# Linear attention into a gated MLP on one core: a quarter of the hidden layer by seven half products in four more blocks, with the kv and numerator steps moved around it

## The chip, the core and the metric

The kernel runs on one core of a Trainium2 chip. The metric is the device time of one execution in microseconds. Five engines run side by side, each with its own queue in program order: TensorE (PE, its weight loads shown as PEld), VectorE (DVE), ScalarE (ACT), GpSimd (POOL) and SyncE (SP, which here only issues DMAs).

## What is computed

```python
# q, k, v: (8, 8, 576, 64); phi(x) = (x if x > 0 else exp(x) - 1) + 1
kv  = einsum('bhsd,bhse->bhde', phi(k), v)   # per batch and head
num = phi(q) @ kv ; den = phi(q) @ sum_s phi(k) + 1e-6
x   = (num / den) as (4608 tokens, 512)
h   = x @ w_in                        # (4608, 2048)
g   = h * sigmoid(beta * h)
out = g @ w_out                       # (4608, 512), float32
```

## The kernel before

**Blocks.** The 8 batches are taken one after the other. Of each batch's 576 tokens 512 make a block (blocks 0 to 7); the 64 left over go into `xT_tail`, and the eight remainders make block 8. Blocks 0 and 1 are prepared by a written-out prologue. From block 1 on a loop (L1012) runs, per block, an H stage (x times w_in, with Silu into `g_sb`) and then a Y stage (`y_fast`, L904: g times w_out). While block b is in these stages, the attention part of later batches is slipped in between: the loop puts functions into two lists, `sh` for the H stage and `sy` for the Y stage, under the number of the step behind which they run (`at`, `run`, L714 to L719). The order of the instructions on each engine is what this program writes; nothing reorders it.

**The H stage.** The 2048 hidden columns are 16 column blocks `ff` of 128, four to a quarter. `h_phase` (L737, blocks 1 to 6) computes each by four matmuls of 512 tokens (`h_mm`, L395) into one PSUM bank (pool of 4, tag "h"), and ScalarE's Silu (`silu`, L408) empties it. `h_fast` (L805, blocks 7 and 8) computes quarters 0 and 2 otherwise (`products`, L817): the 512 x 512 x 512 product of a quarter is split in halves in all three directions and done with seven half products instead of eight, Strassen's scheme in Winograd's form. Each half product is four matmuls of 256 columns. It needs sums of weight halves (`h_w_sums`, L778, four DVE operations per quarter, once), sums of x halves (`h_x_sums`, L792, four DVE operations per block), and six DVE operations per quarter on the results: copy of the first product (L841), two additions that build on it (L844, L845), c2's upper half (L850), hc's upper half (L855) and c2's lower half (L856). The seven products stand in three parts, each behind one plain column block; `hc` is a tile of two PSUM banks (pool "w", two such tiles), `hz` another; the sums that ScalarE reads lie in `hc` and in `c2`.

**The Y stage.** `y_fast` does out = g w_out by seven half products as well (pa twice, pd twice, pc, pb twice; 16 matmuls of 256 columns each). It needs `g_diff` (L721) and `g_sums` (L725) on DVE from the H stage. Its chain on DVE: u2 = pc + r1 (L968), u3 = pd + u2 (L969), y2 = pb + u3 (L978), y2 = pd + u2 (L981), y1 = pb + u2 (L989). The second product into pd accumulates onto the bank that u3 reads, the second into pb onto the bank that y2 reads. The steps of `sy` run at L961 to L999: step 1 behind the first pd product, step 3 behind u3, step 6 at the end.

**Attention for later batches.** `kv_both(n)` (L212) is 72 small matmuls and one DVE copy; `numer_all(n)` (L318) is 72 small matmuls, then four groups of three DVE operations that write x into `xs_sb` (`evac`, L339), and four transposing DMAs on SP's queue from `xs_sb` to `xT` (`trans`, L352). In blocks 3 to 6 they stand at steps 1 and 4 of the H stage, in block 2 at steps 2 and 5. `tail_copy` (L366, POOL) copies the last 64 tokens of a landed `xT`. `next_loads` (L1001, POOL) issues the loads of v, q and k two batches ahead. In the Y stage phi of q (steps 0 and 1) and of k (steps 3 and 4) of batch b + 2 are made by ScalarE's exponential, DVE's `phi_relu` (L165, into an "r" tile, four buffers) and `phi_min` (L173); `q_trans_dma` (step 1) transposes phi of q through SP's queue.

Of the kernel before, what the change touches and what calls it, by code (L numbers as in the profile page):

```python
# [16 lines left out]
def kernel(  # L17
# [145 lines left out]
        st[b, a, pr, "e"] = e  # L163

    def phi_relu(b, a, pr, x):  # L165
        r = work.tile([P, 2, J, D], BF16, tag="r", name="r", bufs=4)
        nc.vector.tensor_scalar(r, x, 0.0, 1.0, ALU.max, ALU.add)
        st[b, a, pr, "r"] = r

    def phi_tile(b, a):  # L170
        st[b, a] = work.tile([P, 2, J, P], BF16, tag=f"phi{a}", name=f"phi_{a}", bufs=1)
# [542 lines left out]
    def run(side, n):  # L714
        for f in side.get(n, ()):
            f()
# [20 lines left out]
    def h_phase(b, x, side):  # L737
        for ff in range(FC):
# [15 lines left out]
                g_parts(b, ff)  # L754


    h_w = vf.rearrange("p i j d -> p (i j d)").bitcast(BF16)
    h_ws = [
        [h_w[:, (4 * n + k) * 512 : (4 * n + k + 1) * 512].rearrange("p (i f) -> p i f", i=2)
         for k in range(4)] for n in range(2)  # L760
    ]
    h_xs = [
        [xq[n].rearrange("p i j d -> p (i j d)")[:, k * 512 : (k + 1) * 512].rearrange(
            "p (i n) -> p i n", i=2) for k in range(4)] for n in range(2)
    ]
    h_c2 = xk[0].rearrange("p i j d -> p (i j d)").bitcast(F32)[:, 0:1024].rearrange(
        "p (t n) -> p t n", t=2
    )
    h_u = [
        xk[1].rearrange("p i j d -> p (i j d)").bitcast(F32)[:, n * 512 : (n + 1) * 512]  # L770
        for n in range(2)
    ]

    def h_w_plain(fq, f, r):

# [1 line left out]

    def h_w_sums(fq):  # L778

        s, a = h_ws[fq // 2], lambda f, r: h_w_plain(fq, f, r)  # L780
        nc.vector.tensor_add(s[0], a(1, 0), a(1, 1))
        nc.vector.tensor_sub(s[1], s[0], a(0, 0))
        nc.vector.tensor_sub(s[2], a(0, 0), a(1, 0))
        nc.vector.tensor_sub(s[3], a(0, 1), s[1])

    def h_x_plain(b, r, t):

# [1 line left out]
            return xT_tail[:, :, 4 * t : 4 * t + 4, r]  # L789
        return xT[b % 2][:, :, 4 * t + r : 4 * t + 4 : 2]  # L790

    def h_x_sums(b):  # L792

        t = h_xs[b % 2]
        x = lambda r, t: h_x_plain(b, r, t)

        def like(a, c):
            return a.rearrange("p i (t n) -> p i t n", n=c.shape[-1])

        for k, (u, w) in enumerate((  # L800
            (x(0, 1), x(0, 0)), (x(1, 1), t[0]), (x(1, 1), x(0, 1)), (x(1, 0), t[1])
        )):
            nc.vector.tensor_sub(like(t[k], u), u, like(w, u) if k % 2 else w)

    def h_fast(b, x, side):  # L805
        run(side, 0)
        hps_of = {}

        def plain(ff):
            hps_of[ff] = bank("h_ps")  # L810
            h_mm(x, ff, hps_of[ff])

        def act(*ffs):
            for ff in ffs:
                silu(b, ff, hps_of[ff])

        def products(fq):  # L817
            s, t = h_ws[fq // 2], h_xs[b % 2]
            cw, z = banks("hc"), banks("hz")[:, 0]
            c2 = h_c2  # L820

            def product(ps, lhs, rhs, first):
                for a in range(2):
                    for i in range(2):
                        o = ps[:, a * 256 : (a + 1) * 256]
                        m = rhs[:, i]
                        if len(m.shape) > 2:
                            o = o.rearrange("p (t n) -> p t n", n=m.shape[-1])
                        nc.tensor.matmul(  # L829
                            o, lhs[:, i, a * P : (a + 1) * P], m,  # L830
                            start=(first and a == 0 and i == 0), stop=True,
                            skip_group_check=True,
                        )

            def w(f, r):
                return h_w_plain(fq, f, r)

            def part1():
                z6 = bank("hz")
                product(z6, s[1], t[1], True)  # L840
                nc.vector.tensor_copy(h_u[0], z6)  # L841
                product(cw[:, 0], w(0, 0), h_x_plain(b, 0, 0), True)
                product(z, s[2], t[2], True)
                nc.vector.tensor_add(h_u[0], cw[:, 0], h_u[0])  # L844
                nc.vector.tensor_add(h_u[1], z, h_u[0])  # L845

            def part2():
                product(cw[:, 1], s[0], t[0], True)
                product(cw[:, 0], w(0, 1), h_x_plain(b, 1, 0), False)
                nc.vector.tensor_add(c2[:, 1], cw[:, 1], h_u[1])  # L850

            def part3():
                product(cw[:, 1], s[3], h_x_plain(b, 1, 1), False)
                product(z, w(1, 1), t[3], False)
                nc.vector.tensor_add(cw[:, 1], cw[:, 1], h_u[0])  # L855
                nc.vector.tensor_add(c2[:, 0], z, h_u[0])  # L856

            def out(n, parts=range(2)):

                for a in parts:  # L860
                    ff = 4 * fq + 2 * n + a
                    src = (cw, c2)[n][:, :, a * 256 : (a + 1) * 256]
                    nc.scalar.activation(
                        g_sb[b % 2][:, ff].rearrange("p (t n) -> p t n", t=2), src,
                        ACTF.Silu, scale=beta_c[:, ff : ff + 1],
                    )

            return part1, part2, part3, out

        plain(4)  # L870
        act(4)
        p1, p2, p3, out = products(0)
        p1()
        plain(5)
        act(5)
        p2()
        plain(6)
        act(6)
        p3()
        out(0)  # L880
        plain(7)
        act(7)
        out(1)
        plain(12)
        act(12)
        p1, p2, p3, out = products(2)
        p1()
        g_diff(b, slice(0, 4))
        plain(13)
        act(13)  # L890
        p2()
        g_diff(b, slice(4, 8))
        plain(14)
        act(14)
        p3()
        out(0, [0])
        plain(15)
        act(15)
        out(0, [1])
        out(1)  # L900
        g_sums(b, 4, 8)
        g_sums(b, 0, 4)

    def y_fast(b, side):  # L904
# [47 lines left out]

        r1 = work.tile([P, 512], F32, tag="r1", name="r1", bufs=1)
        u2 = work.tile([P, 512], F32, tag="u2", name="u2", bufs=1)
        u4 = work.tile([P, 512], F32, tag="u4", name="u4", bufs=1)
        u3 = work.tile([P, 512], F32, tag="u3", name="u3", bufs=1)
        if b < B - 2:
            table(ACTF.Exp)
# [53 lines left out]
    for b in range(1, B + 1):  # L1012
# [3 lines left out]
            at(sh, 0, lambda: tail_copy(b))  # L1016
        if n < B:
            at(sh, 0, lambda: next_loads(n))
            at(sh, {1: 9, 2: 2}.get(b, 1), lambda: kv_both(n))
            at(sh, {1: 11, 2: 5}.get(b, 4), lambda: numer_all(n))  # L1020
        if b == 1:
            at(sh, 4, lambda: w_sum(2))
            at(sh, 9, lambda: w_sum(1))
# [1 line left out]
        if m < B:  # L1025
# [12 lines left out]
            else:  # L1038
# [2 lines left out]
                at(sy, 1, lambda: q_trans_dma(m))  # L1041
                at(sy, 3, lambda: phi_part(m, "k", 0))
                at(sy, 4, lambda: phi_part(m, "k", 1), lambda: table(ACTF.Silu))
        if b == B - 2:
            at(sh, 0, lambda: h_w_sums(0))
            at(sh, 2, lambda: h_w_sums(2))
            at(sy, 0, lambda: h_x_sums(B - 1))
        if b == B - 1:
            at(sy, 0, lambda: h_x_sums(B))
        (h_phase if b < B - 1 else h_fast)(b, xT[b % 2] if b < B else xT_tail, sh)  # L1050
        y_fast(b, sy)


# [28 lines left out]
```

## Time and profile before

| | us |
|---|---|
| median of 3 runs (275.02 to 275.17) | 275.16 |
| the profiled execution, whole | 275.76 |
| its span in the trace | 274.0 |
| H stages of blocks 3, 4, 5, 6 | 15.56, 15.52, 15.61, 15.62 |
| H stages of blocks 7, 8 | 13.36, 13.35 |
| Y stage of each of blocks 2 to 7 | 12.23 |

The granted TensorE clock is 0.999. A timeline row gives the start in us, the length, engine, line, operation, output and inputs by the program's names, shapes, the number of instructions that were merged, and in brackets the idle time of the engine before it with what ended it. Ends of matmuls are modelled, so a row's length runs past the start of the next; distances from start to start are what is used below.

### The profile page before, as it was taken

The numbers are of one execution on the slowest core, as the hardware profiler recorded it, in microseconds if no ns is written. First come the engines' busy times: TensorE is split into PE (matmuls) and PEld (weight loads), VectorE is DVE, ScalarE is ACT, GpSimd is POOL, SyncE is SP. The second block draws the span as 40 slices with busy tenths as digits, with TensorE's granted clock in tenths as the row PEclk, the third lists the DMA queues.
The fourth block names the chain that finished last, engine by engine and source line by source line (L and its number), as shares of the span: only waits on it lengthen the run. The fifth ranks groups of instructions, "written<-read, shape, count | busy, mean of one in ns | idle before, by whom it ended". The sixth has DMA issues, their size and how long they took to land.

```text
span 274.0 us, 6637 instructions
## 1 busy us (share of the span) xinstructions
PE 266.0 (97%) x2809; PEld 176.6 (64%) x2809; DVE 187.8 (69%) x362; ACT 171.3 (63%) x237; POOL 45.8 (17%) x64
## 2 busy tenths in 40 slices
PE   7899998999999999999999999999999999999994
PEld 2575454445865487548754885488548866886793
DVE  4871785999895677566857684677866467856862
ACT  4838877976777776589457945795573047416710
POOL 5932102043014031230113002310000000000000
PEclk9999999999999999999999999999999999999999
DMA  7999999557998996994599659985531060023013
GB/s 253 237 206 350 257 385 255 174 102 228 217 114 176 292 153 119 289 209 73 95 273 223 84 91 261 235 93 87 156 65 24 2 153 0 2 54 101 0 42 115
DMA packets 48958, 42.78 MB, mean 156 GB/s; under 512 B 30352, under 2 KB 40736, under 8 KB 48928
## 3 DMA queue, kind: packets, MB, share of 16 engines
q0 software_dynamic: 13040, 23.40, 36.9%
q1 hardware_dynamic: 35568, 18.75, 33.2%
q8 instruction: 22, 0.36, 0.5%
q10 hardware_dynamic: 320, 0.20, 0.2%
q14 instruction: 8, 0.07, 0.1%
HBM read 36.71 MB, written 9.44 MB: 168 GB/s over the span
## 4 chain that ended last, share of the span: by engine, by line
PE 79%; DMA 13%; DVE 3%; POOL 1%; issue 1%; ACT 0%; DVEq 0%; POOLq 0%
PE h_ps L401 35%; PE ya L944 10%; PE yd L944 10%; PE yb L944 9%; DMA vf<-in_v_dram 8%; PE yc L944 5%; DMA w_in<-in_moe_w_in_dram 4%; PE kvp L222 2%; PE hc L829 2%; PE nps L332 2%; PE hz L829 2%; DMA stage<-in_q_dram 1%; PE yb L916 1%; PE y_ps L416 1%; POOL vf L99 1%
## 5 line engine op out<-in xcount | busy, mean ns | idle before, releaser
L409 ACT ACTIVATE g<-h_ps,beta_c 128x512 bf16<-128x512 f32 x128 | 86.4, 688 | 62.1 <-PE h_ps L401 62.1
L401 PE MATMUL h_ps<-xT,w_in 128*128 128x512 bf16 (+1 forms) x528 | 108.8, 360 | 0.2
L401 PEld LDWEIGHTS <-w_in 128*128 128x128 bf16 x560 | 51.0, 98 | 52.6 <-issue 0.5
L944 PEld LDWEIGHTS <-stage 128*128 128x128 bf16 x480 | 46.9, 98 | 5.6 <-issue 0.2
L944 PEld LDWEIGHTS <-g 128*128 128x128 bf16 x384 | 37.5, 98 | 6.0
L944 PE MATMUL ya<-w_out,g 128*128 128x256 bf16 x256 | 30.6, 273 | 0.0
L727 DVE TENSOR_TENSOR stage<-g 128x1024 bf16<-128x1024 bf16 x16 | 11.2, 697 | 16.3 <-ACT g L409 16.3
L240 POOL CAST vaug<-vf 128x1152 bf16<-128x1152 f32 x11 | 13.9, 1293 | 41.0 <-DMA vf<-in_v_dram 27.9
L347 DVE TENSOR_TENSOR xs_sb<-nps,rden 128x448 bf16<-128x448 f32 (+2 forms) x24 | 18.2, 758 | 0.8
L162 ACT ACTIVATE e<-xk 128x1152 bf16<-128x1152 bf16 (+1 forms) x15 | 16.7, 1160 | 3.1 <-DMA xk<-in_k_dram 3.1
L723 DVE TENSOR_TENSOR stage<-g 128x1024 bf16<-128x1024 bf16 x16 | 12.1, 758 | 8.1 <-ACT g L409 8.1
L162 ACT ACTIVATE e<-xq 128x1152 bf16<-128x1152 bf16 x14 | 15.6, 1159 | 2.7 <-DMA xq<-in_q_dram 2.7
L155 ACT ACT_TABLE_LOAD x12 | 15.4, 1283 | 0.2
L944 PE MATMUL yc<-ws,stage 128*128 128x256 bf16 x128 | 15.3, 273 | 0.0
L944 PE MATMUL yd<-ws,stage 128*128 128x256 bf16 x128 | 15.3, 273 | 0.0
L944 PE MATMUL yd<-ws,g 128*128 128x256 bf16 x128 | 15.3, 273 | 0.0
L416 PE MATMUL y_ps<-w_out,g 128*128 128x512 bf16 x64 | 15.1, 379 | 0.0
L174 DVE TENSOR_TENSOR phi_q<-e,r 128x1152 bf16<-128x1152 bf16 x16 | 12.1, 763 | 3.7 <-ACT e L162 3.0
L367 POOL COPY xT_tail<-xT 128x256 bf16<-128x256 bf16 x6 | 3.6, 608 | 64.5 <-DMA xT<-xs_sb 64.5
L174 DVE TENSOR_TENSOR phi_k<-e,r 128x1152 bf16<-128x1152 bf16 x16 | 12.8, 804 | 1.4
L944 PE MATMUL yb<-ws,stage 128*128 128x256 bf16 x112 | 13.4, 273 | 0.0
L944 PE MATMUL yb<-w_out,stage 128*128 128x256 bf16 x112 | 13.4, 272 | 0.0
(126 smaller groups left out, 303.0 us busy)
## 6 DMA issues: line engine op xcount, KB each, us to landing
vf<-in_v_dram POOLq DMA_DIRECT2D x7, 1152.0 KB, 9.4
out_dram<-y SPq DMA_DIRECT2D x29, 256.0 KB, 3.9
xq<-in_q_dram POOLq DMA_DIRECT2D x7, 576.0 KB, 12.5
xk<-in_k_dram POOLq DMA_DIRECT2D x7, 576.0 KB, 15.4
w_in<-in_moe_w_in_dram POOLq DMA_DIRECT2D x4, 512.0 KB, 12.1
g<-in_moe_w_out_dram POOLq DMA_DIRECT2D x2, 1024.0 KB, 17.2
stage<-in_moe_w_out_dram POOLq DMA_DIRECT2D x2, 1024.0 KB, 21.4
stage<-in_q_dram SPq DMA_DIRECT2D x2, 576.0 KB, 4.5
```

The costliest lines, as they stand in the source:

```text
L155: nc.scalar.activation(act0, warm[:, 0:1], func)
L162: nc.scalar.activation(e, x, ACTF.Exp)
L174: nc.vector.tensor_tensor(st[b, a][:, pr].rearrange("p j (h d) -> p j h d", h=2), st[b, a, pr, "e"].rearrange("p h j d -> p j h d"), st[b, ...
L240: eng.tensor_copy(dst, src)
L347: nc.vector.tensor_mul(xs_sb[:, ils, v0 * D : v1 * D].rearrange("p i (u d) -> p i u d", d=D), pv[:, :, :, 0:D], rden[:, :, :, None].to_bro ...
L401: nc.tensor.matmul(hp[:, c0:c1].rearrange("p (t n) -> p t n", n=n), w_in_sb[ff // 4][:, kc, (ff % 4) * P : (ff % 4 + 1) * P], xm, start=(k ...
L409: nc.scalar.activation(g_sb[b % 2][:, ff, :], hp, ACTF.Silu, scale=beta_c[:, ff : ff + 1])
L416: nc.tensor.matmul(yp[:, c0:c1], g_sb[b % 2][:, ff, t * P : (t + 1) * P], w_out_sb[i][:, c, c0:c1], start=(ff == 0), stop=(ff == FC - 1), ...
L723: nc.vector.tensor_sub(gs[2][:, c], g[:, c, 0:HM], g[:, c, HM:512])
L727: nc.vector.tensor_add(gs[0][:, c], g[:, c, HM:512], g[:, c2, HM:512])
L829: nc.tensor.matmul(o, lhs[:, i, a * P : (a + 1) * P], m, start=(first and a == 0 and i == 0), stop=True, skip_group_check=True,)
L944: nc.tensor.matmul(ps[:, p * HM : (p + 1) * HM], lhs(c, p), rhs(c), start=(first and p == 0 and c == 0), stop=True, skip_group_check=True,)
```

## The change

In blocks 3 to 6 quarter 0 of H is also done by seven half products: `h_fast` now serves blocks 3 to 8, and for blocks below 7 it goes on with plain column blocks 8 to 15. The kv step moves to step 0 (behind plain column block 4, ahead of the products), the numerators to step 8. The sums of x halves move from `xq` into `xs_sb`; they are made in blocks 2 to 7 for the next block, in Y steps 1 and 6 (blocks 2 to 5) or 0 (6 and 7). The weight sums of quarter 0 get a tile of their own and are made in block 2, those of quarter 2 in block 6's Y stage. `c2` and `h_u` come from the pool of "r" tiles, of which there are now two, each twice as large. One half product moves from part 2 to part 3, in all blocks; one g difference in blocks 7 and 8 moves behind part 2, the other behind part 3.

```diff
     def phi_relu(b, a, pr, x):
-        r = work.tile([P, 2, J, D], BF16, tag="r", name="r", bufs=4)
+        if pr == 0:
+            st[b, a, "r"] = work.tile([P, 2, 2, J, D], BF16, tag="r", name="r")
+        r = st[b, a, pr, "r"] = st[b, a, "r"][:, pr]
...
+    h_w = {
+        0: consts.tile([P, 4, 2, 256], BF16, name="h_w0"),
+        2: vf.rearrange(...)...
+    h_xs = xs_sb.rearrange("p i n -> p (i n)")[:, 0:2048].rearrange(
+        "p (k i n) -> p k i n", k=4, i=2
     )
+    def h_room(name):
+        t = work.tile([P, 2, 2, J, D], BF16, tag="r", name=name)
...
             def part2():
                 product(cw[:, 1], s[0], t[0], True)
-                product(cw[:, 0], w(0, 1), h_x_plain(b, 1, 0), False)
                 nc.vector.tensor_add(c2[:, 1], cw[:, 1], h_u[1])
             def part3():
+                product(cw[:, 0], w(0, 1), h_x_plain(b, 1, 0), False)
                 product(cw[:, 1], s[3], h_x_plain(b, 1, 1), False)
                 product(z, w(1, 1), t[3], False)
...
     def h_fast(b, x, side):
-        run(side, 0)
         plain(4)
         act(4)
-        p1, p2, p3, out = products(0)
+        run(side, 0)
+        p1, p2, p3, out = h_products(b, 0)
...
         out(1)
+        if b < B - 1:
+            for ff in range(8, FC):
+                plain(ff)
+                act(ff)
+                run(side, ff)
+                if ff == 9:
+                    g_diff(b, slice(0, 4))
+                    g_diff(b, slice(4, 8))
+                if ff in (11, 15):
+                    g_sums(b, ff - 11, ff - 7)
+            return
...
         p1()
-        g_diff(b, slice(0, 4))
         plain(13)
         act(13)
         p2()
-        g_diff(b, slice(4, 8))
+        g_diff(b, slice(0, 4))
         plain(14)
         act(14)
         p3()
         out(0, [0])
+        g_diff(b, slice(4, 8))
...
-            at(sh, {1: 9, 2: 2}.get(b, 1), lambda: kv_both(n))
-            at(sh, {1: 11, 2: 5}.get(b, 4), lambda: numer_all(n))
+            at(sh, {1: 9, 2: 2}.get(b, 0), lambda: kv_both(n))
+            at(sh, {1: 11, 2: 5}.get(b, 8), lambda: numer_all(n))
...
+        if b == 2:
+            at(sh, 2, lambda: h_w_sums(0))
         if b == B - 2:
-            at(sh, 0, lambda: h_w_sums(0))
-            at(sh, 2, lambda: h_w_sums(2))
-            at(sy, 0, lambda: h_x_sums(B - 1))
-        if b == B - 1:
-            at(sy, 0, lambda: h_x_sums(B))
-        (h_phase if b < B - 1 else h_fast)(b, xT[b % 2] if b < B else xT_tail, sh)
+            at(sy, 0, lambda: h_w_sums(2))
+        if 2 <= b < B:
+            for i, step in enumerate((1, 6) if b < B - 2 else (0, 0)):
+                at(sy, step, lambda i=i, n=n: h_x_sums(n, range(2 * i, 2 * i + 2)))
+        (h_phase if b < 3 else h_fast)(b, xT[b % 2] if b < B else xT_tail, sh)
```

## The prediction, made before the changed kernel was run

> **What bounds the kernel now.** I read the page's engine line first, then the windows by stage, then the timelines of the stages that the change touches.
>
> ```profile
> PE 266.0 (97%) x2809; PEld 176.6 (64%) x2809; DVE 187.8 (69%) x362; ACT 171.3 (63%) x237; POOL 45.8 (17%) x64
> PE 79%; DMA 13%; DVE 3%; POOL 1%; issue 1%; ACT 0%; DVEq 0%; POOLq 0%
> ```
>
> TensorE is busy 97% of the span and carries 79% of the chain that ended last. So a microsecond counts only if it is taken from PE's stream or put in as a hole in it; VectorE (69%) and ScalarE have room on average, but PE waits for them at single points. The windows by stage (core 0; length, then busy time of PE, PEld, DVE, ACT, POOL):
>
> ```profile
> 107.62:123.18 15.56, 15.56 (x211) 7.55 (x209) 9.08 (x20) 10.30 (x15) 5.12 (x6) 1.00 1.01 229
> 123.18:135.41 12.23, 12.23 (x113) 10.96 (x112) 9.14 (x15) 8.97 (x12) 0.58 (x1) 1.00 0.55 91
> 218.85:232.21 13.36, 13.26 (x91) 8.59 (x88) 9.72 (x15) 7.41 (x12) 0.00 (x0) 1.00 0.31 79
> ```
>
> These are block 3's H stage and y stage, and block 7's H stage. PE has no hole in block 3, at full clock; in block 7 it has one of 0.1 us and smaller ones that the modelled ends cover. I write S for the start of a block's H stage and Y for the start of its y stage.
>
> **What the seven products save.** From PE's timeline of block 7:
>
> ```profile
> 221.02 1.03 PE L401 MATMUL h_ps<-xT,w_in 128*128 128x512 bf16 x4
> 221.89 0.60 PE L829 MATMUL hc<-xq,vf 128*128 128x256 bf16 x4
> 222.32 0.60 PE L829 MATMUL hc<-xT,w_in 128*128 128x256 bf16 x4
> 222.76 1.03 PE L401 MATMUL h_ps<-xT,w_in 128*128 128x512 bf16 x4
> 223.70 0.60 PE L829 MATMUL hc<-xT,vf 128*128 128x256 bf16 x4
> ```
>
> Start to start, one column block of four 512-wide matmuls takes 0.864 us (216 ns each), and a product of four 256-wide ones 0.437 (109 each). A quarter of H costs 4 x 0.864 = 3.456 now and 7 x 0.437 = 3.056 after: 0.40 us saved per block if nothing waits, 1.60 over four. The 28 weight loads at 98 ns stay under 28 x 109 ns.
>
> The Trainium skill ("TensorE: Matmul & The Clock Gate", Back-to-back issue gap) speaks against this: it gives a sustained 131 ns per matmul at 512 columns and 81 at 128. By it 16 plain matmuls would cost 2.10 us, and 28 of 256 columns at least 2.27, so each block would lose 0.17 or more. The rows have 216 and 109 ns, and they decide.
>
> **The hole in the third part.** The two numbers that matter are in DVE's timeline of the same stretch:
>
> ```profile
> 220.35 0.69 DVE L841 COPY xk<-hz 128x512 f32<-128x512 f32 x1 [0.61 <-PE hz L829]
> 221.14 0.69 DVE L844 TENSOR_TENSOR xk<-hc,xk 128x512 f32<-128x512 f32 x1
> 221.94 0.69 DVE L845 TENSOR_TENSOR xk<-hz,xk 128x512 f32<-128x512 f32 x1
> 222.96 0.69 DVE L850 TENSOR_TENSOR xk<-hc,xk 128x512 f32<-128x512 f32 x1 [0.33 <-PE hc L829]
> ```
>
> The three chained operations follow each other every 0.79 us; the fourth (c2's upper half) waits 0.33 for the product at 222.32, since it is written behind it. It ends at 223.65, and PE's first product of part 3 starts at 223.70 instead of 222.76 + 0.864 = 223.62: a hole of 0.08. Moving that product into part 3 frees the fourth operation to start at 221.94 + 0.79 = 222.73 and end at 223.42. But in the built order of the changed program it is the moved product that now carries the wait for this operation: both halves of hc are one tile, and the product writes the tile that the operation reads. It is wanted one product earlier: at 222.32 + 0.864 = 223.19, and starts at 223.42 + 0.05 = 223.47. The hole is 0.28, not 0.08: 0.20 worse. In the second quarter the hole is 0.27 already (a g difference on DVE stands between the third and the fourth operation; PE's product starts at 230.48 instead of 230.21); the change moves that difference away and leaves 0.28. So blocks 7 and 8 lose 2 x (0.20 + 0.015): **+0.43**. Bounds: if the wait costs nothing, both holes vanish, 2 x (0.08 + 0.27) = -0.70; if DVE is late by one more of its 0.69 us operations, +1.4 per block. I take the chain of rows.
>
> In blocks 3 to 6 the same chain counts from the first product's start (its fourth operation ends 3.71 us after it, the moved product is wanted after 3.47): a hole of 0.28. Net saving 0.40 - 0.285 = 0.115 per block, **-0.46** for four.
>
> **The rest of the H stage, blocks 3 to 6.** The kv group (0.74 to 0.83 plus 0.09 ahead of it) and the numerators (0.76 plus 0.1) are only moved on PE. ScalarE falls behind: in block 7 its Silu after the eight column blocks starts 2.95 us after the first output of the products; here that is S + 10.21, end S + 10.90, and PE wants that bank for column block 11 at S + 11.08. Column block 10 wants the numerators' first bank at S + 10.21; DVE gives it back 1.52 us after the numerators' start (85.98 to 87.50 in block 2), at S + 10.16. Both fit, with 0.1 us; if that is lost, a tenth or two per block. DVE gets 6 operations of 0.69 and 4 of 0.42, 5.8 us more per block on some 18.3: room, but in a fixed order. The g sums end about Y + 3.5 instead of Y + 3.0, which ScalarE's exponentials hide (phi_q's first waits for them until Y + 4.0, 127.15). The pooled r tiles that now also hold c2 and h_u are written and read on DVE in order, and ScalarE has read c2 long before phi reuses it: nothing. POOL's and SP's queues keep their order in the built program; the transposes are issued later, but ahead of qTd's at Y + 6.1, and DVE's g differences, now behind the numerators, end before Y, where pd needs them at Y + 1.75.
>
> **Where DVE meets the transposes.** This is the main term. The sums of x for the next block stand on DVE in y step 1, behind phi_q and ahead of u2, and in the built order the first of them waits for all four transposes of that xT. Until now only POOL's tail copy waited for them, and nobody waited for POOL. In block 2 the numerators stay at step 5, and the landing can be read off; timelines of DVE, POOL and PE:
>
> ```profile
> 101.49 0.76 DVE L174 TENSOR_TENSOR phi_q<-e,r 128x1152 bf16<-128x1152 bf16 x1
> 102.58 0.69 DVE L968 TENSOR_TENSOR u<-yc,r 128x512 f32<-128x512 f32 x1 [0.33 <-PE yc L944]
> 103.30 0.69 DVE L969 TENSOR_TENSOR u<-yd,u 128x512 f32<-128x512 f32 x1
> ```
>
> ```profile
> 104.05 0.57 POOL L367 COPY xT_tail<-xT 128x256 bf16<-128x256 bf16 x1 [5.93 <-DMA xT<-xs_sb]
> ```
>
> ```profile
> 104.12 1.91 PE L944 MATMUL yd<-ws,g 128*128 128x256 bf16 x16
> 105.88 1.91 PE L944 MATMUL yb<-w_out,stage 128*128 128x256 bf16 x16
> ```
>
> The transposes were issued from 90.01 on, and the last landed at 94.7 + 9.2 = 103.9. DVE is free for the sums at 102.2 and now stands until 104.05. Then two sums (0.46 + 0.34 in block 6's rows) put u2 at 104.85 instead of 102.58, and u3 at 105.57, ending 106.26. PE's second yd product accumulates onto what u3 reads: 106.31 instead of 104.12, a hole of 2.19. Behind it DVE does phi_k (0.56 + 0.67) and y2, which ends at 108.09, so yb starts at 108.14 instead of 105.88. Block 3 starts 2.26 us late: **+2.26**, once. The h_w sums added to block 2 (4 operations, 1.55 us, behind kv_q at 83.42) end at 85.4; the numerators' first operation is at 86.44 with only a 0.6 us difference between, so they move nothing. Bounds: the sums would cost nothing if the landing came before 101.7; a landing as late as the longest issue-to-landing shown (11.3, for the second of the four) would make it 4.3.
>
> In blocks 3 to 5 the landing moves too. The numerators start at S + 8.59 instead of S + 5.25, the first transposes are issued 4.0 later, at S + 12.6. Alone (block 6: 200.48, POOL's copy at 207.12) they take 6.6 us: S + 19.25. Beside the loads of v, q and k they took 9.25 to 10.2 (117.04 to 126.29; 144.80 to 154.73; 172.64 to 182.88). The loads' packets end at about S + 15.8 in block 4, so later transposes meet the loads for 3 us where they met them for 6.4: I take S + 20.5. With Y = S + 15.4, DVE reaches the sums at Y + 6.0 = S + 21.4, and u2 waits for yc until Y + 7.19; with 0.8 us of sums, a landing up to S + 21.7 costs PE nothing. I put 0 and keep S + 22.8 as the other end (up to 1.2 a block). Block 6 has no loads and no phi: 0.
>
> **Sum against the profiled execution:** 275.76 + 2.26 - 0.46 + 0.43 = 278.0. That execution stood 0.6 above the median of the runs (275.16), so I forecast **277.4**. A measurement of this kernel can tell about 0.2%, 0.55 us, from no change.
>
> **Rivals.**
> 1. *Blocks 3 to 5 wait for their transposes too.* If these take the 9.25 to 10.2 of before, they land at S + 21.9 to 22.8 and cost 0.2, 0.9 and 1.2 us: 279.7. For it: DMA is full in H stages (1.01 in the window above). Against it: the loads end before the transposes are half through. Chance 0.16.
> 2. *Block 2's wait is not there* (not slower). It needs xT(3) landed by 101.7, 2.3 us sooner than in this execution: then holes and savings cancel, 275.2. For it: DMA times vary. Against it: the loads of block 2 are issued at the same times as before. Chance 0.09.
> 3. *The saving comes through whole* (faster): PE does not wait for c2's upper half, and rival 2 holds: 275.2 - 1.60 - 0.70 = 272.9; with only the holes gone and block 2's wait there, 277.4 - 4 x 0.285 - 0.43 - 0.70 = 275.1. Chance 0.06 in all, half of it the latter.
> 4. *The change does not do what it says:* excluded, the built order has 28 half-width matmuls in place of 16 in four blocks.
>
> **Numbers.** My forecast with its own range of 276.6 to 278.2 has 0.62; the rest, 0.07, are small waits in the H stages, +1 to +2. The range of 8 in 10 takes the forecast and rival 1 with the lower edge at no change: 275.8 to 279.8. Faster by over 0.2%: 0.04 (rival 3's first half and a little); same: 0.11 (rival 2, rival 3's second half); slower: 0.85.
>
> **What would show it.** Block 2's y stage 14.5 us instead of 12.23, with DVE's first sum of x idle 1.8 us for DMA xT, and the second yd product behind DVE's u3. H stages of blocks 3 to 6 at 15.4 to 15.5; blocks 7 and 8 at 13.6. PE's moved product starting 0.28 late, released by DVE's c2 operation. POOL's tail copies of blocks 4 to 6 before Y + 6. I am wrong if u2 of block 2 starts at its old time, if y stages of blocks 3 to 5 lengthen, or if column blocks 10 and 11 wait for banks.

## The result, and the profile after

The changed kernel takes 277.05 us (median of 11 runs, 276.04 to 279.66); the kernel before takes 275.17 in the same comparison (11 runs, 274.94 to 275.87). The ratio is 1.0076, 95% interval 1.0054 to 1.0097: slower, by about 1.9 us. The forecast was 277.4, range 275.8 to 279.8. The profiled execution took 277.56, its span is 275.8, its clock 0.998. The runs of the changed kernel lie much farther apart than those of the kernel before; the two longest, 279.18 and 279.66, are also the two with a mean granted clock of 0.994 and 0.992. The last section comes back to this.

The busy time of each engine, and the chain of work that ended last by engine:

```profile
PE 264.2 (96%) x2857; PEld 180.4 (65%) x2857; DVE 209.0 (76%) x402; ACT 168.6 (61%) x237; POOL 45.3 (16%) x64
PE 75%; DVE 11%; DMA 6%; ACT 4%; issue 1%; SPq 1%; DVEq 0%
```

TensorE is busy 1.8 us less than before (264.2 against 266.0), so the products do save work, and yet the span is 1.8 us longer. The difference is idle time of PE: VectorE and DMA now hold 17% of the chain that ended last, where they held 16%, and VectorE alone 11% where it held 3%. The windows say in which stages (block 2's Y stage, block 3's H stage, block 7's H stage; length, then busy time of PE, PEld, DVE, ACT, POOL, then clock, DMA share, GB/s):

```profile
94.91:109.54 14.63, 12.47 (x113) 10.94 (x112) 10.78 (x18) 9.18 (x12) 3.55 (x5) 1.00 0.86 135
109.54:124.96 15.42, 15.29 (x223) 8.64 (x221) 11.94 (x26) 9.59 (x15) 3.31 (x4) 1.00 0.99 233
220.07:233.71 13.64, 13.35 (x91) 8.58 (x89) 9.22 (x14) 7.41 (x12) 0.00 (x0) 1.00 0.28 79
```

Block 2's Y stage went from 12.23 to 14.63, block 3's H stage from 15.56 to 15.42, block 7's from 13.36 to 13.64. In the first of them PE is idle for 2.16 of 14.63 us, at full clock. The whole account, from the starts of the stages on PE:

| stages | before | after | difference | predicted |
|---|---|---|---|---|
| Y of block 2 | 12.23 | 14.63 | +2.40 | +2.26 |
| H of blocks 3 to 6 | 62.31 | 61.61 | -0.70 | -0.46 |
| H of blocks 7 and 8 | 26.71 | 27.28 | +0.57 | +0.43 |
| H of block 2 | 15.73 | 15.83 | +0.10 | 0 |
| other Y stages | 12.23 each | 12.23 each | 0 | 0 |
| sum | | | +2.37 | +2.23 |

(Block 2's H stage began 0.58 us earlier in this execution than in that of before, at 79.08 against 79.66, so the spans differ by 1.8 only. H of block 2 varied between 15.66 and 15.90 over the kernels below, with the added weight sums and without, so its +0.10 says nothing.)

The long wait, in VectorE's timeline (start, length, engine, line, operation, shapes, and in brackets the idle time ahead and what ended it):

```profile
100.24 0.76 DVE L175 TENSOR_TENSOR phi_q<-e,r 128x1152 bf16<-128x1152 bf16 x1
103.62 0.43 DVE L805 TENSOR_TENSOR xs_sb<-xT 128x512 bf16<-128x512 bf16 x1 [2.63 <-DMA xT<-xs_sb]
104.09 0.50 DVE L805 TENSOR_TENSOR xs_sb<-xT,xs_sb 128x512 bf16<-128x512 bf16 x1
104.51 0.68 DVE L982 TENSOR_TENSOR u<-yc,r 128x512 f32<-128x512 f32 x1
105.22 0.69 DVE L983 TENSOR_TENSOR u<-yd,u 128x512 f32<-128x512 f32 x1
```

and in TensorE's, with block 3's third part further down:

```profile
101.90 1.91 PE L959 MATMUL yb<-ws,stage 128*128 128x256 bf16 x16
105.96 1.91 PE L959 MATMUL yd<-ws,g 128*128 128x256 bf16 x16 [2.16 <-DVE u L983]
107.80 1.91 PE L959 MATMUL yb<-w_out,stage 128*128 128x256 bf16 x16
...
113.85 1.03 PE L402 MATMUL h_ps<-xT,w_in 128*128 128x512 bf16 x4
115.01 0.60 PE L820 MATMUL hc<-xT,w_in 128*128 128x256 bf16 x4
```

DVE has nothing to do for 2.63 us, since its queue is in order and its head waits for the transposes into xT. u2 and u3, which need no transpose, stand behind it, and PE's second product into yd stands behind u3: 4.06 us after the product before it instead of 1.74 (102.38 to 104.12 in before). The last two lines show the small hole: a plain column block takes 0.864, so the moved product was wanted at 114.71 and starts at 115.01.

### The profile page after: what moved, and what is told of

Its sections match the earlier page's. It is cut to its first block, busy times and chain, and to the rows that moved or that the text cites. A ratio compares the mean times of both kernels' runs of the same rounds, so it can differ in the third digit from the quotient of the medians.

```text
span 275.8 us, 6774 instructions
## 1 busy us (share of the span) xinstructions
PE 264.2 (96%) x2857; PEld 180.4 (65%) x2857; DVE 209.0 (76%) x402; ACT 168.6 (61%) x237; POOL 45.3 (16%) x64
## 4 chain that ended last, share of the span: by engine, by line
PE 75%; DVE 11%; DMA 6%; ACT 4%; issue 1%; SPq 1%; DVEq 0%
PE h_ps L402 28%; PE yd L959 10%; PE ya L959 9%; PE yb L959 8%; PE yc L959 4%; PE y_ps L417 4%; DMA xT<-xs_sb 4%; PE hc L820 3%; DMA stage<-in_k_dram 3%; PE kvp L223 2%; DVE c L840 2%; ACT g L854 2%; PE nps L333 2%; ACT g L410 2%; DVE h_u L835 2%; DVE h_u L836 2%
## 5 line engine op out<-in xcount | busy, mean ns | idle before, releaser
L410 ACT ACTIVATE g<-h_ps,beta_c 128x512 bf16<-128x512 f32 x112 | 74.5, 689 | 60.9 <-PE h_ps L402 60.5
L402 PE MATMUL h_ps<-xT,w_in 128*128 128x512 bf16 (+1 forms) x464 | 96.2, 357 | 0.1
L402 PEld LDWEIGHTS <-w_in 128*128 128x128 bf16 x496 | 45.0, 98 | 43.0 <-DVE xs_sb L348 1.1
L241 POOL CAST vaug<-vf 128x1152 bf16<-128x1152 f32 x11 | 13.3, 1239 | 37.4 <-DMA vf<-in_v_dram 37.4
L854 ACT ACTIVATE g<-hc,beta_c 128x512 bf16<-128x512 f32 x16 | 10.3, 685 | 9.8 <-DVE hc L846 9.8
L728 DVE TENSOR_TENSOR stage<-g 128x1024 bf16<-128x1024 bf16 x16 | 11.3, 709 | 2.1 <-ACT g L410 1.8
## 6 DMA issues: line engine op xcount, KB each, us to landing
xk<-in_k_dram POOLq DMA_DIRECT2D x7, 576.0 KB, 14.6
```

Source lines behind the costliest of these rows:

```text
L241: eng.tensor_copy(dst, src)
L402: nc.tensor.matmul(hp[:, c0:c1].rearrange("p (t n) -> p t n", n=n), w_in_sb[ff // 4][:, kc, (ff % 4) * P : (ff % 4 + 1) * P], xm, start=(k ...
L410: nc.scalar.activation(g_sb[b % 2][:, ff, :], hp, ACTF.Silu, scale=beta_c[:, ff : ff + 1])
L728: nc.vector.tensor_add(gs[0][:, c], g[:, c, HM:512], g[:, c2, HM:512])
L854: nc.scalar.activation(g_sb[b % 2][:, ff].rearrange("p (t n) -> p t n", t=2), src, ACTF.Silu, scale=beta_c[:, ff : ff + 1],)
```

## Experiments

The theory has three terms that do not touch each other: block 2's wait for transposes, the hole ahead of part 3 in all fast quarters, and a saving of 0.40 per quarter that comes whole where nothing waits. The rivals blame other parts of the change. All stage lengths are starts on PE in one profiled execution; times are medians with the kernel before on the same chip.

**The product back in part 2.**

```diff
 def part2():
     product(cw[:, 1], s[0], t[0], True)
+    product(cw[:, 0], w(0, 1), h_x_plain(b, 1, 0), False)
     nc.vector.tensor_add(c2[:, 1], cw[:, 1], h_u[1])
 def part3():
-    product(cw[:, 0], w(0, 1), h_x_plain(b, 1, 0), False)
```

> The changed kernel with the moved half product back in part 2, ahead of c2's upper half, in all six blocks; all else as changed. Chain theory: the hole of 0.30 us ahead of part 3 shrinks to 0.08 per quarter (and the second quarters of blocks 7 and 8, which also had 0.33, to 0.08). H stages of blocks 3 to 6 go from 15.4 to 15.2, those of blocks 7 and 8 from 13.64 to 13.17, the time from 277.05 to 275.2. Rival (the seven products save little because PE is slowed elsewhere in these stages, by contention or by kv ahead of them, and the hole is incidental): H stages stay at 15.4, the time stays within 0.4 of 277.

Measured: H stages of blocks 3 to 6 15.17 to 15.21 instead of 15.39 to 15.42, of blocks 7 and 8 13.24 instead of 13.64 (13.17 was expected). So the moved product costs 0.22 in each of blocks 3 to 6 and 0.40 in each of blocks 7 and 8. The time, 276.06 against 275.98 (ratio 1.0009, 0.9972 to 1.0047), would not have told it; the stages do. Block 2's Y stage was 16.19 here, and why belongs to the last section.

**Block 2's first two sums of x later.** In block 2 alone they stand behind both halves of phi_k and the first addition into y2 (Y step 4) instead of ahead of u2.

```diff
-            for i, step in enumerate((1, 6) if b < B - 2 else (0, 0)):
+            for i, step in enumerate(((4, 6) if b == 2 else (1, 6)) if b < B - 2 else (0, 0)):
```

> The changed kernel with the first two sums of x of block 2 at Y step 4, behind the last phi_k operation, in place of step 1. Chain theory: the Y stage of block 2 goes from 14.63 back to 12.23, no DVE operation ahead of u2 waits for xT, the time goes to 274.7, and the runs spread less than the 276.0 to 279.7 of the changed kernel. Rival (the hole in block 2 comes from DVE's added work as a whole): only the 0.8 us of the two sums moves out of the way, the Y stage stays above 13.5, the time is 276.3 or more.

Measured: Y of block 2 back at 12.23, H of blocks 3 to 8 and the other Y stages as in the changed kernel, 275.96 against 275.98 (1.0004, 0.9976 to 1.0032). The runs spread by 2.0 us, as those of before do on this chip (2.1), so the smaller spread that was expected shows only against the changed kernel's 3.6, which was not measured beside it. VectorE's timeline of the same place, in this kernel:

```profile
100.50 0.76 DVE L175 TENSOR_TENSOR phi_q<-e,r 128x1152 bf16<-128x1152 bf16 x1
102.29 0.69 DVE L982 TENSOR_TENSOR u<-yc,r 128x512 f32<-128x512 f32 x1 [1.03 <-PE yc L959]
...
106.69 0.42 DVE L805 TENSOR_TENSOR xs_sb<-xT 128x512 bf16<-128x512 bf16 x1
```

u2 waits for its product alone and the sums no longer wait for anything. One number in the order of the work was worth 2.4 us in these profiles; that term is shown.

**Part 3 with its z product first**, so that DVE has 0.44 us more to free `hc`; and, as a second kernel, the same with c2's Silus put behind column block 8 in blocks 3 to 6 (second diff).

```diff
 def part3():
+    product(z, w(1, 1), t[3], False)
     product(cw[:, 0], w(0, 1), h_x_plain(b, 1, 0), False)
     product(cw[:, 1], s[3], h_x_plain(b, 1, 1), False)
-    product(z, w(1, 1), t[3], False)
-    nc.vector.tensor_add(cw[:, 1], cw[:, 1], h_u[0])
     nc.vector.tensor_add(c2[:, 0], z, h_u[0])
+    nc.vector.tensor_add(cw[:, 1], cw[:, 1], h_u[0])
```

```diff
         plain(7)
         act(7)
-        out(1)
...
                 plain(ff)
                 act(ff)
+                if ff == 8:
+                    out(1)
```

> The changed kernel with part 3 in another order: the product into hz first, then the moved one, then the other into hc; on DVE c2's lower half ahead of hc's upper half. Chain theory: the product into hz does not need c2's upper half, so the hole of 0.30 ahead of part 3 goes in all eight quarters. But the Silu of hc now starts about 0.15 later while PE comes 0.3 earlier, and in blocks 3 to 6 column block 11 then waits about 0.3 for the bank of column block 8: H stages of blocks 3 to 6 stay at 15.4, those of blocks 7 and 8 go from 13.64 to 13.0; time 275.8. Rival (banks are not short there, the margin of 0.1 us that I worked out is wrong): H stages of blocks 3 to 6 fall to 15.1 too, time 274.6.

> As the kernel with the product into hz first, and in blocks 3 to 6 the two Silus of c2 moved behind the Silu of column block 8. Chain theory: nothing is waited for in the H stages any more; blocks 3 to 6 at 15.1, blocks 7 and 8 at 13.0, block 2's wait for xT unchanged; time 274.6. If the H stages of blocks 3 to 6 come out equal to those of the kernel without this move, ScalarE's lateness was not the reason there.

Measured, z first: blocks 7 and 8 13.02 instead of 13.64, both holes gone; blocks 3 to 6 15.40 to 15.43, unchanged; 276.93 against 275.98 (1.0029, 0.9987 to 1.0070). With the Silus moved: 15.33 to 15.36; 277.96 (1.0052, 1.0012 to 1.0092). In blocks 3 to 6 the hole did not vanish, it moved, but not to the place that I had named. PE and ScalarE of the second kernel in block 4:

```profile
148.47 0.83 PE L333 MATMUL nps<-kv_q,qTd 64*64 64x65 bf16 x72
149.48 2.75 PE L402 MATMUL h_ps<-xT,w_in 128*128 128x512 bf16 x12 [0.18 <-ACT g L410]
```

```profile
147.59 1.26 ACT L854 ACTIVATE g<-hc,beta_c 128x512 bf16<-128x512 f32 x2 [1.36 <-DVE hc L847]
148.74 1.27 ACT L410 ACTIVATE g<-h_ps,beta_c 128x512 bf16<-128x512 f32 x2
```

The numerators need 0.76, so column block 9 could start at 149.23 and starts at 149.48. It wants the bank of column block 7, whose Silu (148.74 to 149.43) stands behind the two Silus of `hc`, not behind those of c2; moving c2's out of the way gave 0.07 us per block and left this wait. My expectation for the second kernel fell there. What it leaves: with z first, DVE's operation on `hc` is its last, ScalarE starts later, and PE meets ScalarE instead of DVE.

**The moves alone:** the kernel before with kv at step 0 and numerators at step 8.

```diff
-            at(sh, {1: 9, 2: 2}.get(b, 1), lambda: kv_both(n))
-            at(sh, {1: 11, 2: 5}.get(b, 4), lambda: numer_all(n))
+            at(sh, {1: 9, 2: 2}.get(b, 0), lambda: kv_both(n))
+            at(sh, {1: 11, 2: 5}.get(b, 8), lambda: numer_all(n))
```

> The kernel before with only the kv step moved to step 0 and the numerators to step 8 of the H stage in blocks 3 to 6; no products, no sums of x there. My theory (moved PE work costs nothing by itself, the transposes land some 4 us later but only POOL's tail copy waits for them): H stages of blocks 3 to 6 15.5 to 15.7, Y stages 12.23, time equal to the kernel before within 0.3 us. Rival (the later transposes run into the q transposes of the Y stage or into the next block's H, and the moved numerators hold up PE): Y stages of 12.4 or more or H stages of 15.9 or more, 1 us or more in all.

Measured: H stages 15.52, 15.52, 15.50, 15.49 (before 15.56, 15.52, 15.61, 15.62), Y stages 12.23; 274.89 against 275.13 (0.9994, 0.9985 to 1.0002). The moves cost nothing and even give 0.07 per block: the kv group takes 0.84 from start to start in before's block 6 and 0.71 here.

**The third part alone:** the kernel before with only the edit of blocks 7 and 8.

> The kernel before with only the change to the last two blocks: the product moved into part 3, the g differences behind part 2 and part 3. Nothing else is touched. My theory (the moved product waits for DVE's c2 operation since it writes the tile that this reads): H stages of blocks 7 and 8 13.64 as in the changed kernel instead of 13.36, 0.57 us in all, a ratio of 1.002. Rival (in the changed kernel the 0.28 per stage came with the new tiles for c2, h_u and the sums, not with the moved product): 13.36 stays and the time is that of the kernel before within 0.1 us.

Measured: 13.63 and 13.64, 275.94 against 275.73 (1.0012, 0.9992 to 1.0032; the total alone is unclear, the stages are not). TensorE of that kernel in block 7's second quarter:

```profile
228.72 1.03 PE L401 MATMUL h_ps<-xT,w_in 128*128 128x512 bf16 x4
229.90 0.60 PE L829 MATMUL hc<-xT,w_in 128*128 128x256 bf16 x4 [0.16 <-DVE xk L849]
```

The hole of 0.32 is there with the old tiles too (c2 still lies in `xk`), so the new tiles have no part in it.

**What beats both.** Product back in part 2 for blocks 3 to 6, part 3 with z first (as above) for blocks 7 and 8, first sums of x at step 4 in blocks 2 to 5.

```diff
 def part2():
     product(cw[:, 1], s[0], t[0], True)
+    if b < B - 1:
+        product(cw[:, 0], w(0, 1), h_x_plain(b, 1, 0), False)
...
-            for i, step in enumerate((1, 6) if b < B - 2 else (0, 0)):
+            for i, step in enumerate((4, 6) if b < B - 2 else (0, 0)):
```

> The changed kernel with three edits: in blocks 3 to 6 the moved product is back in part 2; in blocks 7 and 8 part 3 begins with the product into hz, so that DVE's c2 operation has 0.44 us more before hc is written; in blocks 2 to 5 the first two sums of x stand behind the exponential of k (Y step 4) instead of ahead of u2. My theory (three independent terms: block 2's wait 2.40, the hole ahead of part 3 in blocks 3 to 6 0.22, in blocks 7 and 8 0.6): H stages of blocks 3 to 6 15.2, of blocks 7 and 8 13.02, Y of block 2 12.23; against the kernel before 4 x 0.38 + 2 x 0.33 = 2.2 us less, so a ratio of 0.992 and about 273.0 where before takes 275.2. Rival (the terms are not independent: what is saved in an H stage is given back in the next Y stage, where DVE is late by then): Y stages of blocks 3 to 5 become 12.4 to 12.8 and the ratio stays above 0.996. A second rival, that the clock and not the holes makes the difference in the runs: then this kernel's runs spread by 3 us too, as those of the changed kernel do; by my theory they agree within 1 us wherever those of the kernel before do.

Measured: 273.31 (273.07 to 273.83) against 275.13 (274.82 to 275.60), ratio 0.9941, interval 0.9929 to 0.9953. Windows of block 2's Y, block 3's H, block 7's H and block 7's Y:

```profile
95.30:107.54 12.24, 12.24 (x113) 10.95 (x112) 9.93 (x16) 9.17 (x12) 2.29 (x3) 1.00 1.07 154
107.54:122.75 15.21, 15.21 (x223) 8.64 (x220) 12.46 (x27) 9.59 (x15) 4.68 (x6) 1.00 0.90 217
217.26:230.28 13.02, 13.02 (x90) 8.60 (x88) 9.48 (x15) 6.97 (x11) 0.00 (x0) 1.00 0.30 82
230.28:242.67 12.39, 12.39 (x113) 10.97 (x112) 8.88 (x16) 4.12 (x7) 0.00 (x0) 1.00 0.01 1
```

The terms do add up: 15.51 with the moves alone less 15.20 is 0.31 a block, the 0.40 of the seven products less the hole of 0.08 that the old order has. The first rival (given back in the Y stages of blocks 3 to 5) is out, they are 12.23. The gain is 1.8 us and not the 2.2 expected; 0.16 of the difference is a new wait in block 7's Y stage, 12.39 instead of 12.23 in the last line: with z first the last Silus come later, ScalarE's copy of `ya` ends at 233.90 behind them, and the second product into `ya` starts at 233.94 instead of 233.78. Block 8's Y stage has the same wait once more (the copy ends at 259.31, the product starts at 259.36 instead of 259.19). With both, the stages give 1.50 + 0.67 - 0.33 = 1.84 us, which is what the medians have. The second rival, on the clock, is out as far as this chip tells: the five runs lie within 0.8 us, as those of before do, with mean clocks of 0.997 to 1.000.

## Why the prediction was right

**Block 2's wait (predicted +2.26, measured +2.40).** The mechanism and nearly the size. The landing was taken from POOL's tail copy, at Y + 8.66 in before; DVE's first sum started at Y + 8.71. Its two sums took 0.89 from the first's start to u2, not the 0.80 of block 6's rows. The landing 0.05 later and the sums 0.09 longer make the 0.14. DVE was idle for 2.63 us and not for the 1.8 that was named as a sign, since it came to the sums earlier (the last phi_q starts at Y + 5.33, at Y + 6.10 in before); the landing ends the wait, so this cost nothing. That the size came out within 0.14 is in part luck: in the six other profiles with this wait, all shown below, the first sum starts between Y + 8.11 and Y + 9.79, so one execution of before could not give the landing to better than about a microsecond. Moving the sums alone (the second experiment) took the whole term away.

**The hole in the third part.** The chain of four DVE operations was said to end 3.71 after the first product's start; in block 7 it ended at 220.94 + 3.71 = 224.65, and the product started at 224.71, wanted at 224.41. Holes of 0.30 and 0.33 where 0.28 was said for both quarters: +0.57 for blocks 7 and 8 instead of +0.43. That PE really waits for a reader of the other half of `hc` is shown by the edit alone in the kernel before, and by the start 0.06 behind the end of that operation. DVE and PE of the changed kernel, block 7:

```profile
223.96 0.69 DVE L840 TENSOR_TENSOR c<-hc,h_u 128x512 f32<-128x512 f32 x1
```

```profile
224.71 0.60 PE L820 MATMUL hc<-xT,w_in 128*128 128x256 bf16 x4
```

**Blocks 3 to 6 (predicted -0.46, measured -0.70).** 0.40 saved and a hole of 0.30 were right; the term that was mis-sized is that the kv group and the numerators are only moved on PE, put at nothing: the move itself is worth 0.07 per block (the experiment with the moves alone), 0.28 of the sum. 15.51 - 0.40 + 0.30 = 15.41, which is what the stages have. The sustained figures of the Trainium skill ("TensorE: Matmul & The Clock Gate", "Back-to-back issue gap"), by which each block would have lost, did not hold here: the steps are 0.864 for four plain matmuls (216 ns each) and 0.437 for four of half width (109) again.

**Transposes in blocks 3 to 5.** Estimated to land at S + 20.5. POOL's timeline of the changed kernel:

```profile
130.30 0.88 POOL L368 COPY xT_tail<-xT 128x256 bf16<-128x256 bf16 x1 [13.29 <-DMA xT<-xs_sb]
...
156.77 0.82 POOL L368 COPY xT_tail<-xT 128x256 bf16<-128x256 bf16 x1 [7.23 <-DMA xT<-xs_sb]
...
185.32 0.40 POOL L368 COPY xT_tail<-xT 128x256 bf16<-128x256 bf16 x1 [6.75 <-DMA xT<-xs_sb]
```

The H stages began at 109.54, 137.19 and 164.83, so these are S + 20.8, S + 19.6 and S + 20.5, ahead of DVE's S + 21.4. Rival 1 did not come. That step was right with 0.6 to 1.8 us to spare, and it is the step that could most easily have gone wrong: the estimate of the collision with the loads rested on one block. There the last packet of the loads ended at S + 17.0 and not at about S + 15.8, which would have meant a longer collision; in the changed kernel the loads of blocks 3 to 5 were done by S + 14.6, 16.1 and 16.4. So the landing was right in part by luck.

**Where I was wrong in a detail.** That column blocks 10 and 11 fit with 0.1 us was not tested in the changed kernel, because the hole ahead of part 3 shifts PE later by 0.30. In the kernels with z first, where that hole is gone, the first to wait is column block 9, on the Silu of column block 7, by 0.25. I had looked for the late bank at the end of ScalarE's queue and not at the first bank wanted after the group that uses none. What the working did not contain at all is the spread of the runs, 3.6 us where before's is 0.9. That it left the median near the forecast is luck as well: two of the eleven runs here have a low mean clock, but three of six on the chip of the last section, where the median is 278.17. And the medians differ by 1.9 us where the stages of the one profiled execution add up to 2.4; the landing varies by more than this difference, and one profile cannot tell the median's.

## What to carry to other kernels

An operation that waits for a transfer should stand in an in-order queue behind everything that does not need that transfer: here two small sums, 0.9 us of work, cost 2.4 us ahead of the operations that PE was waiting for, and nothing three steps later. When a product is moved to let one operation start sooner, look up what its own output tile is waiting for; a write to one half of a tile waited for a reader of the other half. And read the stages, not the totals: three of the terms here are 0.2 to 0.6 us, well shown in the stage lengths and lost in the medians.

## What was not expected: a hole lowers the clock behind it

In some kernels block 2's Y stage was longer than its hole explains. The product back in part 2 had the same hole as the changed kernel (2.14 against 2.16 us), but a Y stage of 16.19 instead of 14.63. Its windows of 2 us, with the granted clock third from the end:

```profile
104.00:106.00 2.00, 0.15 (x2) 0.13 (x2) 1.97 (x4) 1.74 (x3) 0.20 (x1) 1.00 0.80 129
106.00:108.00 2.00, 2.00 (x14) 1.53 (x13) 1.89 (x4) 0.00 (x0) 0.00 (x0) 0.66 0.58 92
108.00:110.00 2.00, 2.00 (x12) 1.34 (x11) 1.36 (x2) 0.00 (x0) 1.67 (x3) 0.50 0.05 12
110.00:112.00 2.00, 2.00 (x18) 1.24 (x18) 0.79 (x2) 0.00 (x0) 1.09 (x2) 0.99 0.75 180
```

PE is busy again from 105.85, and from about 106.6 to 110.0 it runs at half clock: (1 - 0.66) x 2 / 0.5 + 2 + 0.04 = 3.4 us, which would cost 1.7; the stage is 1.6 longer. A first guess, that the load on the chip lowers the clock, was set against the guess that the idle stretch does, by three kernels: PE kept busy in the hole with eight matmuls into an unused bank, the changed kernel again beside it, and the hole made longer.

```diff
+        if b == 2:
+            fill = banks("fill")[:, 0]
+            for _ in range(8):
+                nc.tensor.matmul(fill, warm[:, 0:P], warm, start=True, stop=True)
         run(side, 4)
         product(pd, part(8, 1), wsum(3), False)
```

> The changed kernel with 8 matmuls of 128x512 into an unused bank in block 2's Y stage, between the first product into yb and the second into yd, where PE stands 2.1 to 2.8 us behind DVE's u3. They compute nothing that is used. Theory of the clock (an idle stretch of PE of that length lowers the granted clock for some 3.4 us in some executions): the stage keeps its 14.6 us, since u3 still comes late, but PE's hole shrinks to 0.4 us, the clock stays at 1.00 behind it, and the runs of this kernel agree within about 1 us, with a median at or up to 1 us below the changed kernel's own on this chip. Rival (the clock drops for another reason, which the load on the chip sets): the spread and the drops at 106 to 112 us stay as they are in the changed kernel. Second rival (the eight matmuls delay the product themselves): Y of block 2 becomes 15 us or more.

> The changed kernel as it is, on the same chip as the two others, for its spread: by the theory of the clock its slowest runs lie 1.5 to 3 us above its fastest and the profiled execution, if it is one of those, shows a granted clock of 0.5 to 0.8 in some two to four us behind the hole of block 2's Y stage; by the rival the spread is that of the kernel before.

```diff
-                at(sy, step, lambda i=i, n=n: h_x_sums(n, range(2 * i, 2 * i + 2)))
+                for _ in range(3 if b == 2 and i == 0 else 1):
+                    at(sy, step, lambda i=i, n=n: h_x_sums(n, range(2 * i, 2 * i + 2)))
```

> The changed kernel with block 2's first two sums of x made three times over (the same values written again; nothing is left out), so that DVE comes 1.7 us later to u2 and PE's hole in block 2's Y stage grows from 2.1 to 2.9 to some 3.8 us. Theory of the clock (an idle stretch of PE can lower the granted clock for some 3.4 us, the more surely the longer it is): the half clock behind the hole comes in nearly every execution, Y of block 2 is 17.9 or more (14.63 + 1.7 + 1.6), and the median lies 3 us or more above the changed kernel's fast ones (276.6 to 277.4), at 280 or above. Rival (the clock has nothing to do with the hole's length): clock 1.00 in most executions, Y of block 2 16.3, the median 278.3 to 279.

Measured on one chip: with the filling 277.23 (276.63 to 278.24; ratio 1.0081, 1.0064 to 1.0099), the changed kernel again 278.17 (276.63 to 281.92; 1.0102, 1.0074 to 1.0130). TensorE with the filling, and without it:

```profile
101.57 1.91 PE L959 MATMUL yb<-ws,stage 128*128 128x256 bf16 x16
103.53 1.67 PE L996 MATMUL fill<-warm 128*128 128x512 bf16 x7
105.04 1.91 PE L959 MATMUL yd<-ws,g 128*128 128x256 bf16 x16
```

```profile
103.96 1.91 PE L959 MATMUL yb<-ws,stage 128*128 128x256 bf16 x16
108.75 3.34 PE L959 MATMUL yd<-ws,g 128*128 128x256 bf16 x16 [2.89 <-DVE u L983]
111.89 2.19 PE L959 MATMUL yb<-w_out,stage 128*128 128x256 bf16 x16
```

With the filling (eight of 216 ns, one record is missing) the clock stays at 1.00 and Y takes 14.03, the product starting 0.06 behind the end of u3 as before; without it the hole was 2.89 in the profiled execution, the longest of the six runs, the clock 0.76 from 108 to 110 and 0.50 from 110 to 112, and Y took 16.94. The profile with the filling is a weak test: the transposes landed 0.6 us earlier in it than in the first profile of the changed kernel (first sum at Y + 8.11), and by these rows PE would have stood for 1.7 us only without the filling, less than in any profile with half clock here. Of the six runs of the changed kernel here, the three with a mean clock of 0.993 to 0.994 or less are those above 278.9, the three at 1.0 lie between 276.6 and 277.4. A mean clock lower by 0.006 over 276 us is 1.7 us, one such stretch. With the filling no run is above 278.3, where three of six were, but six runs are few, the two intervals overlap, and one of the filled runs (277.77) has a clock of 0.994 too. Of the spread 1.6 us are left, where I had said 1; a run of 278.24 had clock 1.0, so this part is not the clock's, and what it is stays open (the landing of the transposes varies and would do it).

The longer hole, on another chip: 281.89 (280.16 to 286.11) against 275.73, ratio 1.0202 (1.0164 to 1.0239), all six runs with a mean clock of 0.974 to 0.993. In the profiled execution, the longest of the six, the hole came out at 5.07 us, 1.3 longer than the 3.8 expected (the landing was later as well), the Y stage at 19.94, and block 3's H stage at 16.60 since DVE was still late there. With that hole the rival's median would have been 279.6 to 280.3 (1.3 more than expected), so the median hardly tells the two apart. All six runs have a low clock, where six of 17 of before have on that chip, and the windows of the profile show the half clock behind the hole:

```profile
108.00:110.00 2.00, 0.00 (x0) 0.00 (x0) 1.90 (x5) 0.52 (x2) 0.00 (x0) 0.81 0.88 142
110.00:112.00 2.00, 1.07 (x6) 0.75 (x6) 1.86 (x4) 0.00 (x0) 0.76 (x2) 0.50 0.02 5
112.00:114.00 2.00, 2.00 (x11) 1.44 (x10) 1.90 (x4) 0.00 (x0) 1.75 (x3) 0.50 0.45 67
114.00:116.00 2.00, 2.00 (x11) 1.38 (x10) 0.84 (x2) 0.00 (x0) 0.00 (x0) 0.50 1.02 412
116.00:118.00 2.00, 2.00 (x29) 1.24 (x31) 0.89 (x2) 0.02 (x1) 0.51 (x1) 0.98 1.14 262
```

0.76 + 2 + 2 + 2 + 0.08 = 6.8 us at half clock, the first 1.7 of it still in the hole, and twice the 3.4 seen with the shorter holes: the stretch comes in steps of 3.4.

The hole is not the only thing that lowers the clock. On that chip six of the 17 runs of the kernel before had a mean clock of 0.988 to 0.994, and on a third chip four of the six runs with the sums at step 4, a kernel without the hole, had 0.988 to 0.992, as five of eleven of before had 0.988 to 0.993 there. The profiles show another place: in those of the changed kernel again, of the sums made three times and of the two kernels with z first, 3.4 or 6.8 us at half clock also lie in the prologue, between 13 and 21 us. So a low mean clock of a run without a profile does not say that the hole was its cause. Between the prologue and the last 2 us of the span, half clock stands in four of the twelve profiles, each time in or behind this hole.

The traces also say when it comes. Within the span, all edges of half clock in one execution lie on a grid of 3.413 us: in the changed kernel again at 13.46, 20.29, 109.04, 112.45 and 279.70, which are 2, 26, 1 and 49 such steps apart. The grid does not start with the hole, so the same hole can fall into one step or into two. Here are the changed kernel (its grid from the half clock that starts at 274.76, 50 steps on) and the product back, each in two steps of its own grid:

```profile
100.68:104.09 3.41, 3.12 (x29) 2.65 (x28) 0.75 (x3) 2.76 (x4) 0.47 (x1) 1.00 1.02 157
104.09:107.51 3.42, 1.55 (x15) 1.38 (x15) 3.28 (x6) 1.20 (x2) 0.22 (x1) 1.00 0.61 101
```

```profile
103.23:106.64 3.41, 1.27 (x13) 0.99 (x11) 2.95 (x6) 2.51 (x3) 0.68 (x1) 1.00 0.86 140
106.64:110.05 3.41, 3.41 (x19) 2.35 (x17) 2.72 (x5) 0.00 (x0) 1.72 (x3) 0.50 0.19 34
```

The hole of 2.16 is cut by the grid into 0.29 and 1.87, the one of 2.14 lies in one step, and half clock is the step behind it. What the profiles have together, one execution each:

| kernel | PE's hole, us | most of it in one step of 3.41 us | half clock from the next step on, us | Y of block 2 |
|---|---|---|---|---|
| sums at step 4 | none | none | none | 12.23 |
| hole filled | under 0.1 | under 0.1 | none | 14.03 |
| z first | 1.96 | 1.34 | none | 14.43 |
| changed kernel | 2.16 | 1.87 | none | 14.63 |
| product back | 2.14 | 2.14 | 3.4 | 16.19 |
| z first, Silus moved | 2.80 | 2.14 | 3.4, 0.7 of it in the hole | 16.52 |
| changed kernel again | 2.89 | 2.89 | 3.4 | 16.94 |
| sums made three times | 5.07 | 3.37, then 1.70 | 6.8, 1.7 of it in the hole | 19.94 |

So in these profiles a step of the grid with 1.87 us or less of this hole leaves the clock alone, and one with 2.14 or more is followed by a step at half clock, which cost 1.6 us where PE was busy all through it; whether a hole of about 2.1 us costs this depends on where it falls on the grid, and that differed from profile to profile. The last microseconds, where PE waits as well, agree: a step with 1.70 us idle is not followed by half clock (sums at step 4), one with 2.08 is (product back). In the prologue idle time alone does not sort the steps: some with 0.9 to 1.3 us idle are followed by half clock, others with 1.4 are not, and what else counts there stays open. The Trainium skill ("TensorE: Matmul & The Clock Gate", "Why this matters for your kernels") asks for "No PE-idle gaps >~3µs between matmul bursts", and its section "What's actually happening" has a free-running window of 3413 ns. The length of the steps here, 3.4 us, and their grid agree with that window; the limit of 3 us does not agree, since 2.14 was enough. The phase of the grid was read off, not set: no run here could set it.
